# The head of a four-layer kernel: order of the last turn, the weights' squares and zero passes before the first product

## The chip, the cores and the metric

The kernel runs on one core of a Trainium2 chip. The metric is device time in microseconds (us) of one execution; of the kernel before there are three timed runs, and the median counts. Besides them one execution was profiled, and all rows shown come from it. A core has TensorE (PE, with its weight loads listed as PEld), VectorE (DVE), ScalarE (ACT), GpSimd (POOL) and SyncE (SP), which issues most DMAs. Each engine works through its own instructions in order and waits on semaphores for the others.

## The reference

Two pairs of layers act on x of 2048 tokens by 448 features: attention with 16 heads of 28, then a gated MLP of 1792 columns, and the same two again with the same weights.

```python
x = A_x
x = x + _A_ref(_layernorm(x, axis=-1), A_wqkv, A_wo)
x = x + _B_ref(_layernorm(x, axis=-1), B_w_gate, B_w_up, B_w_down)
x = x + _A_ref(_layernorm(x, axis=-1), A_wqkv, A_wo)
x = x + _B_ref(_layernorm(x, axis=-1), B_w_gate, B_w_up, B_w_down)
```

`_A_ref` multiplies by `wqkv` (448 by 1344), forms softmax(q k / sqrt(28)) v for each head and multiplies by `wo`; `_B_ref` is (sigmoid(x Wg) * (x Wu)) Wd. All inputs are float32.

## The kernel before, in words

The tokens stand as 16 tiles of 128 by 448, in four blocks (`Block`) of four tiles. Every product in the projections is made of float16 parts: an operand is scaled by a power of two, its high part is the rounding to float16 and its low part the rest. A weight matrix and a block of tokens are cut along the 448 features into four slots of 128, 128, 128 and 64 rows. The fourth slot of a block holds its high part in rows 0 to 63 and its low part in rows 64 to 127 (`tail`); the weights' fourth slot holds the same 64 rows twice.

The power of two for a weight matrix comes from its sum of squares. `measure(j)` squares the matrix `j` (0 for the queries' columns, 1 keys, 2 values) on ScalarE and adds along a row into `sums`; `size(j)` adds over the partitions with a product by a matrix of ones on TensorE (the float32 product shows as two matmuls), and `powers` makes the scale `up` from it in two small VectorE instructions (L233, L235). `high_cols` is ScalarE's scaled copy to float16 (L218), `low_cols` is VectorE's rest (L221).

The head, up to the first product, is written out in the order in which each engine gets it. SyncE issues the four tiles of block 0, the first weights in four pieces (slots 0 and 1 together, slot 2, and the 64 rows of slot 3 twice), then the second weights, block 1, the third weights and blocks 2 and 3. Meanwhile `keep_busy` makes products of a zero tile into a bank that nobody reads (L248). For each tile of block 0, `stats` (L435 to L440, VectorE and GpSimd) takes mean and spread, `scale` normalizes it (L283, VectorE) and `turn` transposes it on TensorE into four banks (L448), one for each slot. The first weights are squared in two parts of two slots each (L549), and both parts are added up by `size(0)` (L554, L556), which stands between the last tile's `scale` and its `turn`. Then come `tables()` (constants on GpSimd), the high part of the first 128 columns, `turned_high` (the block's high part out of the banks, ScalarE, L466 and L468), the high part of the other 320 columns, the low part of the first 128, `turned_low` (the block's low part, VectorE, L473 and L476) and one more zero pass.

`project` follows: seven products of 128 columns of queries and keys, each of 11 matmuls (L497) by `by_features`. The 11 terms are (high weights, high block), (high weights, low block) and (low weights, high block) for three slots, and two for the tail. Their order is a list; for the first two of the seven it is another one, since their operands become ready one after another. Behind each of the seven stands one piece of further work from `along`: behind the first `tile0` (the low part of the other 320 columns, `measure(1)`, ones for the values on GpSimd), behind the second `tile1` (`size(1)` and 64 columns of the second weights), then `tile2` (the rest of them), `measure(2)`, `size(2)` and `split_v` (the third weights). Each product is then scaled out of its bank by ScalarE (L673, L676) and VectorE (L674, L678).

## Time and profile before

| | us |
|---|---|
| median of three timed runs | 1931.62 |
| lowest and highest | 1931.43, 1933.78 |
| the profiled execution | 1932.95 |
| its span | 1930.8 |
| TensorE busy in the span | 1915.8 |
| VectorE busy | 1248.2 |
| ScalarE busy | 1314.0 |

A row of the order of time gives the start in the span and the duration in us, the engine, the line, the operation, what it writes and reads, and how many like instructions it stands for; in square brackets stands how long the engine was idle before it and what released it. Rows that group a form give its count, its busy time in us and the mean of one in ns. Rows of waits give the engine and line that waited, for whom, the total in us, the number of times and the longest.

### The profile page before, as it was taken

Reading aid. Unit: us, or ns where it says so; the run is one execution under the profiler, and the core shown is the slowest. Engines: PE = TensorE matmul, PEld = TensorE weight load, DVE = VectorE, ACT = ScalarE, POOL = GpSimd, SP = SyncE. Lnnn points to the kernel's source line nnn. Section 1 sums busy time; section 2 is a strip of 40 time slices with the busy share of each in tenths; the row PEclk is TensorE's granted clock in tenths of the full one; section 3 lists DMA queues with packets and bytes.
Section 4 is the critical chain, followed back from the end, with each engine's and each line's share of the span. In section 5 each row is a group of like instructions: output and inputs, shape, how many; then the busy total and the mean of one; then the engine's idle time right before and its main releaser. Section 6 shows DMA issues by size and latency. Waiting matters only on the chain. (4 is left out here: it accounts for less than half of the span.)

```text
span 1930.8 us, 53585 instructions
## 1 busy us (share of the span) xinstructions
PE 1915.8 (99%) x23392; PEld 1327.5 (69%) x23392; DVE 1248.2 (65%) x2348; ACT 1314.0 (68%) x1574; POOL 164.5 (9%) x308
## 2 busy tenths in 40 slices
PE   8999999999999999999999999999999999999999
PEld 4455555555566777777744568799898777777776
DVE  6638878778676555555574487787778664655543
ACT  5569999999983344444345799999999544343432
POOL 2013322221001000000000000000000000000000
PEclk9999999999999999999999999999999999999999
DMA  5566664334216313232334321122111243333310
GB/s 172 158 197 176 187 195 129 107 102 113 64 62 242 107 69 108 81 128 79 101 111 131 94 51 47 30 51 51 42 36 65 104 169 117 107 111 97 115 49 20
DMA packets 90533, 201.49 MB, mean 104 GB/s; under 512 B 10830, under 2 KB 58030, under 8 KB 90160
## 3 DMA queue, kind: packets, MB, share of 16 engines
q1 hardware_dynamic: 65680, 111.02, 19.7%
q0 software_dynamic: 17776, 83.51, 13.0%
q8 instruction: 185, 3.03, 0.7%
q10 hardware_dynamic: 6832, 3.44, 0.7%
q14 instruction: 60, 0.49, 0.1%
HBM read 142.61 MB, written 47.98 MB: 99 GB/s over the span
## 5 line engine op out<-in xcount | busy, mean ns | idle before, releaser
L1065 ACT ACTIVATE prob_s<-sc 128x1536 f32<-128x1536 f32 x658 | 890.8, 1490 | 8.6 <-PE sc L1050 6.0
L1101 PE MATMUL acc<-prob_s,val_s 128*32 128x256 f32 (+3 forms) x7732 | 591.6, 383 | 0.0
L1050 PE MATMUL sc<-qp_s 114*32 114x512 f16 x7888 | 575.8, 379 | 0.9 <-ACT prob_s L1065 0.9
L512 PEld LDWEIGHTS <-gu_s 128*128 128x128 f16 x4368 | 427.3, 98 | 60.7 <-issue 1.3
L1050 PEld LDWEIGHTS <-qp_s 114*32 114x32 f16 x8192 | 315.8, 95 | 173.0 <-issue 80.0
L1101 PEld LDWEIGHTS acc<-prob_s,val_s 128*32 128x32 f32 x7732 | 321.5, 110 | 96.2 <-issue 7.0
L1354 DVE TENSOR_TENSOR one_q<-side,one_q 128x512 f32<-128x512 f32 x112 | 71.9, 683 | 298.0 <-PE side L512 298.0
L512 PE MATMUL chain<-xwide_s,gu_s 128*128 128x256 f16 x2016 | 247.5, 273 | 0.6 <-ACT one_q L1338 0.5
L1338 ACT COPY one_q<-chain 128x256 f32<-128x256 f32 x224 | 83.0, 372 | 205.5 <-PE chain L512 201.6
L1081 DVE SCALAR_TENSOR_TENSOR power_q<-power_q,expo_q 128x512 f32<-128x512 f32 x228 | 157.8, 692 | 7.8
L1307 PE MATMUL dnp<-dn_s,hhl_q 128*128 128x448 f16 x448 | 157.9, 352 | 0.0
L1308 PE MATMUL dnp<-dn_s,hhl_q 128*128 128x448 f16 x448 | 157.9, 352 | 0.0
L1309 PE MATMUL dnp<-dn_s,hhl_q 128*128 128x448 f16 x448 | 157.9, 352 | 0.0
L512 PE MATMUL side<-xshort_s,gu_s 128*128 128x256 f16 x1120 | 140.9, 272 | 0.0
L497 PE MATMUL qkp<-xhl_s,wqk_s 128*128 128x512 f16 x616 | 139.8, 383 | 0.4 <-ACT xhl_s L466 0.3
L497 PEld LDWEIGHTS <-wqk_s 128*128 128x128 f16 x616 | 60.6, 99 | 71.5 <-issue 2.7
L1130 DVE STREAM_TRANSPOSE oturned_q<-acc 128x512 f32<-128x512 f32 x32 | 22.9, 716 | 130.9 <-PE acc L1101 130.8
L512 PE MATMUL side<-xwide_s,gu_s 128*128 128x256 f16 x672 | 91.7, 273 | 0.0
L1101 PE MATMUL acc<-power_q,val_s 128*32 128x128 f32 (+3 forms) x284 | 88.6, 394 | 0.0
L1338 ACT COPY two_q<-chain 128x256 f32<-128x256 f32 x112 | 41.7, 372 | 67.4 <-PE chain L512 67.4
L1365 ACT ACTIVATE one_q<-one_q 128x512 f32<-128x512 f32 x56 | 35.3, 630 | 59.5 <-DVE one_q L1354 59.5
L1075 DVE TENSOR_SCALAR expo_q<-aside,base 128x512 f32<-128x512 f32 x76 | 56.8, 748 | 28.7 <-PE aside L1050 28.4
(188 smaller groups left out, 2080.0 us busy)
## 6 DMA issues: line engine op xcount, KB each, us to landing
gu_s<-gu_parts POOLq DMA_DIRECT2D x56, 800.0 KB, 4.9
qp_s<-qk_scr SPq DMA_DIRECT2D x96, 224.0 KB
gu_s<-gu_parts SPq DMA_DIRECT2D x20, 800.0 KB
qk_scr<-qkhl_q SPq DMA_DIRECT2D x56, 256.0 KB
gu_parts<-pack_s POOLq DMA_DIRECT2D x14, 800.0 KB, 3.9
xraw_s<-xt_scr SPq DMA_DIRECT2D x12, 768.0 KB
xt_scr<-xs_s SPq DMA_DIRECT2D x34, 224.0 KB
qp_s<-qk_scr SPq DMA_DIRECT2D x64, 112.0 KB
```

The source lines that it names most:

```text
L497: nc.tensor.matmul(pm, w, x, start=(i == 0), stop=(i == len(terms) - 1))
L512: nc.tensor.matmul(pm, a, x, start=(first and i == 0), stop=(i == len(terms) - 1), skip_group_check=True)
L1050: nc.tensor.matmul(ps[32 * j:32 * j + 32, :], hd.k[:, keys], hd.q[:, qb * W:(qb + 1) * W], start=True, stop=True, tile_position=(0, 32 * j))
L1065: nc.scalar.activation(prob[:, 0:n, :], ps[:, 0:n, :], AF.Exp, scale=exp_scale)
L1075: nc.vector.tensor_scalar(y, ps, base2[:, 0:1], -126.0, op0=ALU.mult, op1=ALU.max)
L1081: nc.vector.scalar_tensor_tensor(p, p, c[k], y, op0=ALU.add, op1=ALU.mult)
L1101: nc.tensor.matmul(acc[qb * VC:(qb + 1) * VC, s], v[:, kc % TB, h, :], probs[c * NB + qb][:, s], start=(kc == 0 and a == 0), stop=(kc == N ...
L1307: nc.tensor.matmul(pm, hl[:, 0, s], dw[:, 0, :], start=begin, stop=False)
L1308: nc.tensor.matmul(pm, hl[:, 0, s], dw[:, 1, :], start=False, stop=False)
L1309: nc.tensor.matmul(pm, hl[:, 1, s], dw[:, 0, :], start=False, stop=end)
L1338: nc.scalar.copy(to, pm)
L1354: nc.vector.tensor_tensor(one[m], side[m], one[m], op=ALU.add)
```

## The change

The fourth turn comes ahead of the weights' sums. The first weights' squares are taken in three parts with a column of `first_sums` each: slots 0 and 1 and then slot 2 on ScalarE, slot 3 on VectorE (one instruction that multiplies and adds up, with a read of its accumulator); each part has its own product with the matrix of ones into the same bank. Zero passes stand behind every turn and around the three sums: one behind the fourth turn, three, one and three behind the sums, where one stood behind the last turn. The block's high parts come out of the banks ahead of the scaled weights: slot 0 by VectorE, slots 1 and 2 by ScalarE; the tail follows after the first 128 columns. Those columns are scaled in two steps, slot 0 alone and then the other three, and their low part stands between the block's low parts. The first product's list puts the block's low part of slots 0 and 1 ahead of the low weights, and that of slot 2 behind them. `measure` and `size` lose their special case.

```diff
-    rest = cpool.tile([P, 1], F32, name="rest")
+    first_sums = cpool.tile([P, 3], F32, name="first_sums")
...
-        def turned_high(self):
-            for kt, pt in self.pt.items():
-                if kt < 3:
-                    nc.scalar.copy(self.hi[:, kt, :], pt)
+        def turned_high(self, kts=range(4), engine=None):
+            for kt in kts:
+                if kt not in self.pt:
+                    continue
+                to, pt = ((self.hi[:, kt, :], self.pt[kt]) if kt < 3 else
+                          (self.tail[0:64], self.pt[kt][0:64]))
+                if engine is nc.vector:
+                    nc.vector.tensor_copy(to, pt)
                 else:
-                    nc.scalar.copy(self.tail[0:64], pt[0:64])
+                    nc.scalar.copy(to, pt)
...
         if first_tile == 0:
-            terms = terms[0::3] + terms[2::3] + terms[1::3] + tails
+            terms = terms[0::3] + terms[1:5:3] + terms[2::3] + terms[7:8] + tails
...
+        def measure_first(self, i):
+
+            rows = self.raw[0][:, (slice(0, 2), slice(2, 3), slice(3, 4))[i]]
+            junk = qrt.get("junk", [P, 2, D], BF16)
+            out, to = junk[:, 0:rows.shape[1]], first_sums[:, i:i + 1]
+            if i == 2:
+                nc.vector.tensor_tensor_reduce(out, rows, rows, 1.0, 0.0, op0=ALU.mult,
+                                               op1=ALU.add, accum_out=to)
+            else:
+                nc.scalar.activation(out, rows, AF.Square, accum_out=to)
+            qrt.put(junk)
+
+        def sum_first(self, i):
+            if i == 0:
+                self.first = bank(3, "sums")[:, 0:1]
+            nc.tensor.matmul(self.first, ones, first_sums[:, i:i + 1], start=(i == 0),
+                             stop=(i == 2))
+            if i == 2:
+                powers(0, 1, self.first)
...
-        def high_cols(self, j, c0, c1):
+        def high_cols(self, j, c0, c1, kts=slice(0, 4)):
             c = slice(j * D + c0, j * D + c1)
-            scaled_high(self.qk[0][:, :, c], self.raw[j][:, :, c0:c1], j)
+            scaled_high(self.qk[0][:, kts, c], self.raw[j][:, kts, c0:c1], j)
...
-    wq.measure(0)
+    wq.measure_first(0)
...
         first.scale(t)
-        if t == TB - 1:
-            wq.size(0)
         first.turn(t)
-        if t < TB - 1:
-            keep_busy()
+        keep_busy()
         if t + 2 < TB:
             first.stats(t + 2)
+    wq.sum_first(0)
+    first.turned_high([0], nc.vector)
+    keep_busy(3)
+    wq.measure_first(1)
+    wq.measure_first(2)
+    wq.sum_first(1)
+    first.turned_high([1, 2])
+    keep_busy()
+    wq.sum_first(2)
     tables()
-    wq.high_cols(0, 0, P)
+    keep_busy(3)
+    wq.high_cols(0, 0, P, slice(0, 1))
+    wq.high_cols(0, 0, P, slice(1, 4))
+    first.turned_high([3])
+    wq.high_cols(0, P, D)
+    first.turned_low([0, 1])
+    wq.low_cols(0, 0, P)
+    first.turned_low([2, 3])
     big.put(first.xn)
-    first.turned_high()
-    wq.high_cols(0, P, D)
-    wq.low_cols(0, 0, P)
-    first.turned_low()
-    keep_busy()
```

More of the change, by code (lines that the diff above doesn't have):

```diff
@@ L461, in turn_raw, with turned_low @@
             big.put(self.xn)
-        def turned_high(self):
-            for kt, pt in self.pt.items():
-                if kt < 3:
-                    nc.scalar.copy(self.hi[:, kt, :], pt)
-                else:
-                    nc.scalar.copy(self.tail[0:64], pt[0:64])
-        def turned_low(self):
-            for kt, pt in self.pt.items():
+        def turned_high(self, kts=range(4), engine=None):
[6 more added lines that the diff above has]
+                    nc.vector.tensor_copy(to, pt)
+                else:
+                    nc.scalar.copy(to, pt)
+        def turned_low(self, kts=range(4)):
+            for kt in kts:
+                if kt not in self.pt:
+                    continue
+                pt = self.pt[kt]
                 if kt < 3:
@@ L542, in read @@
             load_rows(self.raw[j], wqkv, j * D, D, parted=(j == 0))
+        def measure_first(self, i):
[15 more added lines that the diff above has]
+                powers(0, 1, self.first)
         def measure(self, j):
             junk = big.get("junk", [P, 4, D], BF16)
-            for s, to in (((slice(0, 2), sums[:, 0:1]), (slice(2, 4), rest)) if j == 0 else
-                          ((slice(0, 4), sums[:, j:j + 1]),)):
-                nc.scalar.activation(junk[:, s], self.raw[j][:, s], AF.Square, accum_out=to)
+            nc.scalar.activation(junk, self.raw[j], AF.Square, accum_out=sums[:, j:j + 1])
             big.put(junk)
         def size(self, j):
-            pb = bank(7 if j else 3, "sums")
-            nc.tensor.matmul(pb[:, 0:1], ones, sums[:, j:j + 1], start=True, stop=(j > 0))
-            if j == 0:
-                nc.tensor.matmul(pb[:, 0:1], ones, rest, start=False, stop=True)
+            pb = bank(7, "sums")
+            nc.tensor.matmul(pb[:, 0:1], ones, sums[:, j:j + 1], start=True, stop=True)
             powers(j, 1, pb[:, 0:1])
-        def high_cols(self, j, c0, c1):
+        def high_cols(self, j, c0, c1, kts=slice(0, 4)):
             c = slice(j * D + c0, j * D + c1)
-            scaled_high(self.qk[0][:, :, c], self.raw[j][:, :, c0:c1], j)
+            scaled_high(self.qk[0][:, kts, c], self.raw[j][:, kts, c0:c1], j)
         def low_cols(self, j, c0, c1):
```

## The prediction

> **What bounds the kernel now.** I read the page's first, second and fourth parts, then the order of time over the first 36 us, then stretches of it with the granted clock.

> ```profile
> span 1930.8 us, 53585 instructions
> PE 1915.8 (99%) x23392; PEld 1327.5 (69%) x23392; DVE 1248.2 (65%) x2348; ACT 1314.0 (68%) x1574; POOL 164.5 (9%) x308
> PE 44%; DVE 0%; ACT 0%; issue 0%; DVEq 0%; ACTq 0%
> ```

> TensorE is busy for 99% of the span and is nearly alone on the chain that ended last. So what reaches the first product earlier, or makes the first products faster, shortens the run by as much, provided no later wait is tied to a fixed time. The execution took 1932.95 us, of which the span is 1930.8; it lies 1.33 above the median of the timed runs, 1931.62.

> The order of time (start, duration, engine, line, operation) shows the front as a relay across four engines:

> ```profile
> 9.61 0.51 DVE L283 TENSOR_SCALAR xn_s<-x,mv,rs 128x448 f32<-128x448 f32 x1 [0.72 <-POOL rs L440]
> 10.52 0.19 ACT L549 ACTIVATION_READ_ACCUMULATOR junk_s<-wraw_s 128x1 f32 x1
> 10.85 0.35 PE L554 MATMUL sums<-sums,ones 128*128 128x1 f32 x2 [1.03 <-POOL ind_f_q L181]
> ...
> 11.40 0.95 ACT L549 ACTIVATE junk_s<-wraw_s 128x896 bf16<-128x896 f32 x1 [0.69 <-DMA wraw_s<-in_A_wqkv_dram]
> 12.49 0.58 PE L556 MATMUL sums<-rest,ones 128*128 128x1 f32 x2 [1.29 <-ACT junk_s L549]
> 12.94 1.09 PE L448 MATMUL turn<-ident,xn_s 128*128 128x128 f32 x4
> 13.11 0.16 DVE L233 TENSOR_SCALAR pw<-sums 128x1 int32<-128x1 int32 x1 [3.00 <-PE sums L556]
> 13.49 0.72 ACT L218 ACTIVATE wqk_s<-wraw_s,up 128x512 f16<-128x512 f32 x1 [1.05 <-DVE up L235]
> 14.12 1.54 ACT L466 CAST xhl_s<-turn 128x512 f16<-128x512 f32 x3
> 14.25 0.75 DVE L221 SCALAR_TENSOR_TENSOR wqk_s<-wraw_s,up,wqk_s 128x512 f16<-128x512 f32 x1 [0.79 <-ACT wqk_s L218]
> 14.74 7.10 PE L497 MATMUL qkp<-xhl_s,wqk_s 128*128 128x512 f16 x22 [0.28 <-ACT xhl_s L466]
> 14.92 1.88 DVE L473 TENSOR_TENSOR xhl_s<-turn,xhl_s 128x512 f16<-128x512 f32 x3
> ...
> 21.68 0.28 PE L554 MATMUL sums<-sums,ones 128*128 128x1 f32 x2
> 21.82 4.91 PE L497 MATMUL qkp<-xhl_s,wqk_s 128*128 128x512 f16 x22
> 22.00 0.16 DVE L233 TENSOR_SCALAR pw<-sums 128x1 int32<-128x1 int32 x1 [0.91 <-PE sums L554]
> ```

> The last piece of the first weights lands at 11.40 (ScalarE waits for it). Square, sum on TensorE, scale on VectorE and ScalarE's scaled copy follow one another; the fourth turn stands behind the sums, at 12.94, though its input was ready at 10.12. The first product starts at 14.74. The first 22 products take 7.10, the next 22 take 4.91. The sums of the second weights at 21.68 stand behind those 22, and all scaling of the second weights hangs on them, so 21.68 is the mark that I move.

> Why 7.10 is seen in stretches (busy us of PE, PEld, DVE, ACT, POOL with instruction counts, granted clock, DMA share, GB/s):

> ```profile
> 5.44:8.85 3.41, 1.74 (x10) 0.97 (x10) 2.69 (x7) 0.00 (x0) 1.82 (x5) 1.00 1.05 311
> 8.85:12.26 3.41, 1.22 (x7) 0.78 (x7) 0.55 (x2) 1.91 (x4) 3.11 (x10) 1.00 1.11 258
> 12.26:15.67 3.41, 2.90 (x9) 1.55 (x10) 1.73 (x5) 2.36 (x7) 2.93 (x8) 0.50 0.99 306
> 15.67:19.08 3.41, 3.41 (x9) 1.13 (x8) 3.35 (x4) 3.40 (x4) 0.60 (x3) 0.50 1.13 324
> 19.08:22.50 3.42, 3.42 (x19) 1.74 (x18) 1.28 (x5) 1.35 (x3) 0.00 (x0) 1.00 1.00 374
> ```

> From 12.26 to 19.08 the clock is half, after a stretch in which TensorE was busy 1.22 of 3.41. The first 4.3 us of products run in it.

> **The change part by part.** Loads are issued in the same order on SyncE and no DMA is added or moved; GpSimd's order is unchanged, since nothing that moved waits for it. The rest is 7 zero passes, one more sum, a smaller split of squares and another order.

> *Squares.* SyncE issues a later load when the third slot's semaphore comes free; the last tail's landing is ScalarE's wait to 11.40.

> ```profile
> 10.40 0.47 SPq L200 DMA_DIRECT2D wraw_s<-in_A_wqkv_dram  x1
> L953 DVE CUSTOM_DVE_ANT_0 junk_s<-raw_s,sums x19: 1144/1284/2085, 146.9 to 223.4; 128x1024 bf16<-128x1024 f32 x14, 128x1792 bf16<-128x1792 f32 x4, 128x896 bf16<-128x896 f32 x1
> L953 DVE DVE_READ_ACCUMULATOR2_ANT part<- 128x1 f32 x19 | 1.6, 82 | 0.0
> ```

> So slot three is there by 10.40, and ScalarE, free at 10.71, squares it then: 896 columns cost 0.95 (at 11.40) and 1792 cost 1.69 (at 17.29, below), so 448 cost 0.58, and with the read it is done at 11.40. The tails go to VectorE from 11.40. Its multiply-and-sum is L953's operation: 1.14 for 896 (the shortest of 19) and 2.08 for 1792, so 0.68 for 448, plus 0.08: ready at 12.16. Before, TensorE had the squares at 12.49. Bounds for the 0.68: 0.5 (the pass over 448 columns at 9.61) to 1.14 (the row of twice the columns).

> *Turn and zero passes.* The turn starts at 10.15 instead of 12.94.

> ```profile
> 1.25 3.60 PE L248 MATMUL still<-still_q 128*128 128x512 f16 x8 [1.25 <-DVE warm L166]
> 8.95 0.65 PE L448 MATMUL turn<-ident,xn_s 128*128 128x128 f32 x4 [0.51 <-DVE xn_s L283]
> 9.44 0.38 PE L248 MATMUL still<-still_q 128*128 128x512 f16 x1
> ```

> At full clock it takes 0.65, with the zero pass from 0.49 on. TensorE keeps order, so everything behind it counts: turn 10.15, pass, first sum (0.35, as at 10.85) to 11.2, three passes at 4.91/22 = 0.22 to 11.87, second sum 12.2, one pass 12.45, third sum. Its data are there at 12.16, so by data VectorE reads it at 12.5 (0.32 from 21.68 to 22.00), by queue at 12.85. I take 12.7. The passes behind it (0.67) end at 13.4, before anything needs TensorE. In the stretch to 12.26 TensorE is now busy for 0.87 + 0.87 + 0.35 + 0.67 + 0.3 = 3.1 of 3.41. The stretch to 8.85 kept the clock with 1.74 of 3.41 us, the next one lost it with 1.22. So I take the full clock as held up to the first product and behind it.

> [...]

> *First product.* Scales and handover: 13.11 to 13.49, 0.38, so ScalarE starts at 13.08. It now scales only the first slot, 128 columns.

> ```profile
> 16.02 1.37 ACT L218 ACTIVATE wqk_s<-wraw_s,up 128x1280 f16<-128x1280 f32 x1
> 16.83 0.68 DVE L476 TENSOR_TENSOR xhl_s<-turn,xhl_s 64x512 f16<-64x512 f32 x1
> 17.29 1.69 ACT L549 ACTIVATE junk_s<-wraw_s 128x1792 bf16<-128x1792 f32 x1
> 17.55 1.55 DVE L221 SCALAR_TENSOR_TENSOR wqk_s<-wraw_s,up,wqk_s 128x1280 f16<-128x1280 f32 x1
> 22.38 0.51 ACT L218 ACTIVATE wqk_s<-wraw_s,up 128x256 f16<-128x256 f32 x1 [1.61 <-DVE up L235]
> ```

> 0.51 for 256 and 1.37 for 1280 give 0.40 for 128: done 13.48. The copy of the turned slots no longer stands between, as VectorE (slot 0, at 10.45, at most the 0.63 of a low part, before the tails land) and ScalarE (slots 1, 2, from 11.4 to 12.4 at 0.51 each) did them while the sums were under way. First product at 13.55, 1.2 earlier. Bounds, with those above: 13.3 to 14.0.

> *The 22 products.* At 0.22 they would take 4.9, but now VectorE sets the pace: from 13.05 two low parts at 0.63, low columns 0.75 (14.25), a third low part 0.63, the tail 0.70: 16.4. ScalarE's part (three slots 0.61, the tail's copy 0.51, then 1.37) ends at 15.7 and does not hold it. The two tail products end at 16.9; seven of the second tile take 1.56, to 18.45, when the low columns (16.4 + 1.55 = 17.95) are there; four more, 19.35. So the second weights' sums come at 19.35 instead of 21.68: **2.3 us**, 1.2 from the earlier start and 1.1 from the products. The full clock alone is worth 2.2 there (half of 14.74 to 19.08); the waits for VectorE take 1.1 of it back.

> *Cover.* The squares of the second weights now start on ScalarE at 15.6 instead of 17.29 and must end by 19.35; they take 1.9, so 1.8 are spare. If their weights landed only at 17.29, the copy of the first tile would be late by 0.4 and nothing else. Everything from 21.68 on hangs on that sum and shifts as a whole. One wait in this stretch is 1.1 long, on VectorE's split of the third weights:

> ```profile
> PE vp L523 <- DVE wv_s L221: 1.1, 1, 1.1
> 26.55 1.68 ACT L549 ACTIVATE junk_s<-wraw_s 128x1792 bf16<-128x1792 f32 x1
> ```

> It follows the products too, so it moves along; it does not shrink.

> *Sum.* 1932.95 - 2.3 = 1930.65 against the profiled execution. How much of its excess over the median is profiling and how much its own half-clock stretch can't be read: if it is all profiling, the median becomes 1929.3; if the timed runs have less half clock, they gain less. I take the middle: **1929.9**.

> **The rivals.**

> *The clock wanders* (part of the forecast's own range). The timed runs differ by 2.35 us among themselves (1931.43 to 1933.78), about the 2.2 that the half clock costs here. In a timed run with the flips up to 2 us later or earlier, the half clock costs the first products 1 us less or more than the 2.2 here (half of 4.3), so the gain is 1.3 to 3.3: 1928.3 to 1930.3 from the median. [...]

> *All waits of the front fall away*: data set the third sum (12.5), the low parts overlap, 22 products take 4.9 from 13.3, and the sums come at 18.2, 3.5 earlier; with half of the 1.1 wait gone too, 4.0: 1927.6. For it: VectorE was idle for 3.0 us ahead of 13.11. Against it: its five pieces add up to 3.3.

> *Slower: the zero passes at half clock.* If the clock is half from 10 us on (it was half at 1.25 to 4.85, 0.43 a pass), the same queue takes: turn 1.09, pass 0.43, sum 0.58, three passes 1.28, sum 0.58, pass 0.43, sum 0.58: third sum read at 15.0, three passes more to 16.3, first product 1.6 later than before. If the clock comes back at 19.08 as before, 6.5 products run at 0.43 and 15.5 at 0.22: 22.5 against 21.68, 1932.4 from the median; it is slower from a return at about 17.3 on. If it never comes back within the 22, 16.3 + 9.4 = 25.7: 4.0 later, 1935.6. Against it: the rows at 8.95 and 9.44 are at full speed, and what falls between them and 10.15 is unchanged.

> *It moves the front and gives it back*: a load at a fixed time. The third weights are squared at 26.55, 24.2 then. The hardware queue's packets and MB, over the first 9 and the first 18 us:

> ```profile
> q1 hardware_dynamic: 1211, 1.96, 77.4%
> q1 hardware_dynamic: 2359, 4.61, 92.1%
> ```

> 1.96 MB had moved by 9 us, and the first 1.835 MB (four tiles of x, 0.917, and the first weights, as much) had landed by 11.40. 4.61 MB by 18 us are the 4.59 up to the third weights, so by the same lag they land at about 21, 3 us early. Should they land at 26.5, up to 2.3 are lost again: 1931.6.

> **How the numbers follow.** Forecast, with the wandering clock: 0.62. All waits gone: 0.12. Slower by the passes: 0.11. Given back: 0.15. A measurement of this kernel tells about 0.2%, 3.9 us, from no change. Beyond it on the fast side is the second case alone, with a little of the first: 0.13; on the slow side half of the third: 0.06; within: 0.81. The forecast's own range is 1928.3 to 1930.7; with the given-back case and the nearer half of the slower one, and cutting the far ends, 1927.9 to 1932.3 leaves out about 2 in 10.

> **What would show it.** The fourth turn at 10.1 to 10.3; a third sum between 12.2 and 12.6; the first product at 13.3 to 13.8; full clock in the stretches to 12.26, 15.67 and 19.08; VectorE without idle time from 13.05 to 18; the sums of the second weights at 19.2 to 19.5; from there every row earlier by the same amount. A half clock in any of these stretches, a multiply-and-sum above 1.2 us, a DMA as the releaser of ScalarE at 15.6, or a longer wait on the third weights' split would make it wrong.

## The result, and the profile after

| | before | after |
|---|---|---|
| median, us | 1932.62 (22 runs, 1931.43 to 1934.1) | 1929.72 (22 runs, 1929.09 to 1932.98) |
| the profiled execution | 1932.95 | 1929.57 |
| its span | 1930.8 | 1927.9 |

The ratio of the times is 0.9986, with a 95% interval of 0.998 to 0.9993: 2.9 us between the medians, about 0.15%, with an interval that leaves out 1. The kernel before was timed again beside the new one, which moved its median from 1931.62 to 1932.62.

The order of time of the changed kernel, the rows that answer to those shown of before (start, duration, engine, line, operation, idle time ahead in brackets):

```profile
8.01 0.95 ACT L560 ACTIVATE junk_q<-wraw_s 128x896 bf16<-128x896 f32 x1 [5.71 <-DMA wraw_s<-in_A_wqkv_dram]
9.74 0.66 PE L448 MATMUL turn<-ident,xn_s 128*128 128x128 f32 x4 [0.35 <-DVE xn_s L283]
10.11 0.69 DVE L470 CAST xhl_s<-turn 128x512 f16<-128x512 f32 x1 [0.42 <-PE turn L448]
10.67 0.81 PE L248 MATMUL still<-still_q 128*128 128x512 f16 x3
10.71 0.61 DVE L557 CUSTOM_DVE_ANT_0 junk_q<-wraw_s 128x448 bf16<-128x448 f32 x1
11.25 0.08 DVE L557 DVE_READ_ACCUMULATOR2_ANT first_sums<- 128x1 f32 x1
11.31 0.28 PE L566 MATMUL sums<-first_sums,ones 128*128 128x1 f32 x2
11.53 0.38 PE L248 MATMUL still<-still_q 128*128 128x512 f16 x1
11.74 0.28 PE L566 MATMUL sums<-first_sums,ones 128*128 128x1 f32 x2
12.06 0.16 DVE L233 TENSOR_SCALAR pw<-sums 128x1 int32<-128x1 int32 x1 [0.72 <-PE sums L566]
12.44 0.91 ACT L218 ACTIVATE wqk_s<-wraw_s,up 128x128 f16<-128x128 f32 x2 [1.15 <-DVE up L235]
12.89 2.46 PE L504 MATMUL qkp<-xhl_s,wqk_s 128*128 128x512 f16 x9
...
15.63 2.97 PE L504 MATMUL qkp<-xhl_s,wqk_s 128*128 128x512 f16 x13 [0.28 <-DVE xhl_s L483]
...
18.43 0.28 PE L578 MATMUL sums<-sums,ones 128*128 128x1 f32 x2
...
32.86 0.35 PE L530 MATMUL vp<-wv_s,xhl_s 128*128 128x448 f16 x1 [1.07 <-DVE wv_s L221]
```

The row of the kernel before that answers to the last one:

```profile
36.11 0.35 PE L523 MATMUL vp<-wv_s,xhl_s 128*128 128x448 f16 x1 [1.08 <-DVE wv_s L221]
```

The fourth turn has moved from 12.94 to 9.74, the first product from 14.74 to 12.89, and the sums of the second weights from 21.68 to 18.43, 3.25 earlier. The span is 2.9 shorter. The wait on the third weights' split is as long as before (1.07 against 1.08) and 3.25 earlier: nothing between was given back. (The span less the start of those sums is 1909.12 before, 1909.47 after, and between 1908.1 and 1909.5 in the other profiles, so the 0.35 is scatter.) Three things in these rows are not the change's doing or not as planned. The first weights' slots were there at 8.01 instead of 9.66, in the same order of loads. The square of the last piece, at 10.71, names no DMA and starts as VectorE ends its copy of slot 0 (10.11): here the weights were no longer what the head waited for (the trace records the last of their transfers as landed at 9.95). And TensorE's queue shows: the last square is read out at 11.33, but the third sum runs at 11.74, behind the second sum and its pass.

Stretches of the changed kernel (busy us of PE, PEld, DVE, ACT, POOL, then the granted clock, DMA share and GB/s):

```profile
8.85:12.26 3.41, 3.06 (x21) 2.19 (x20) 1.91 (x6) 1.83 (x6) 3.20 (x9) 1.00 1.09 309
12.26:15.67 3.41, 2.89 (x13) 0.86 (x12) 3.35 (x7) 3.23 (x5) 2.93 (x8) 1.00 1.01 371
15.67:19.08 3.41, 3.41 (x18) 1.72 (x18) 2.74 (x5) 2.20 (x4) 0.60 (x3) 1.00 1.11 350
```

TensorE is busy for 3.06 of the stretch in which it had 1.22, and the clock stays full, where it was half for 6.82 us.

### The profile page after: what moved, and what is told of

Its sections match the earlier page's. It is cut to its first block, busy times and chain, and to the rows that moved or that the text cites. A ratio compares the mean times of both kernels' runs of the same rounds, so it can differ in the third digit from the quotient of the medians.

```text
span 1927.9 us, 53606 instructions
## 1 busy us (share of the span) xinstructions
PE 1915.1 (99%) x23401; PEld 1297.4 (67%) x23401; DVE 1249.7 (65%) x2351; ACT 1313.1 (68%) x1574; POOL 164.9 (9%) x308
## 5 line engine op out<-in xcount | busy, mean ns | idle before, releaser
L1123 PE MATMUL acc<-prob_s,val_s 128*32 128x256 f32 (+3 forms) x7732 | 582.8, 383 | 0.0
L1072 PE MATMUL sc<-qp_s 114*32 114x512 f16 x7888 | 567.1, 379 | 0.9 <-ACT prob_s L1087 0.9
L1072 PEld LDWEIGHTS <-qp_s 114*32 114x32 f16 x8192 | 295.7, 96 | 188.7 <-issue 91.7
L1123 PEld LDWEIGHTS acc<-prob_s,val_s 128*32 128x32 f32 x7732 | 304.6, 110 | 108.8 <-issue 7.9
```

Of the source, the lines that this page charges most:

```text
L1072: nc.tensor.matmul(ps[32 * j:32 * j + 32, :], hd.k[:, keys], hd.q[:, qb * W:(qb + 1) * W], start=True, stop=True, tile_position=(0, 32 * j))
L1123: nc.tensor.matmul(acc[qb * VC:(qb + 1) * VC, s], v[:, kc % TB, h, :], probs[c * NB + qb][:, s], start=(kc == 0 and a == 0), stop=(kc == N ...
```

## The experiments

Two questions: does the gain come from the held clock, from the order, or from both; and what in the order carries it. Times are medians of 11 runs, each beside runs of the kernel before on the same chip (1932.41 for the first four, 1932.43 for the next four, 1931.94 for the last three). Since loads land at another time in each execution (the last piece of the first weights at 11.40 and 10.32 in two profiles of the kernel before), the profiles are compared by the **lag**: the start of the second weights' sums, less the start of the square that takes the last piece of the first weights. It is 21.68 - 11.40 = 10.28 before and 18.43 - 10.71 = 7.72 after. Where the row of that square names a DMA, the lag starts as the piece lands; where it doesn't (10.71 above, and three more profiles below), VectorE was still at its copy of slot 0, and the piece had landed earlier.

### Without the added passes

```diff
     wq.sum_first(0)
     first.turned_high([0], nc.vector)
-    keep_busy(3)
...
-    keep_busy()
     wq.sum_first(2)
     tables()
-    keep_busy(3)
```

> The changed kernel without its seven added zero passes; the pass behind the fourth turn stays. Theory (earlier start and held clock each carry part of the 2.9 us): the fourth turn still comes ahead of the sums, but the clock falls to half between 11 and 13 us, the sums take 0.58 instead of 0.28, the first product starts 0.3 to 0.6 later than with the passes and some ten products run at 0.43, so 1.5 to 2.5 us are lost: 1931.2 to 1932.2. Rival A (the clock carries everything): 1932.6, as before. Rival B (order alone carries it, the passes are idle): within 0.3 of 1929.7, with full clock up to the first product.

Measured: 1930.57 (1929.55 to 1932.21), ratio 0.9988 [0.9979, 0.9997]. Its order of time and its stretches:

```profile
11.45 0.63 DVE L557 CUSTOM_DVE_ANT_0 junk_q<-wraw_s 128x448 bf16<-128x448 f32 x1 [1.00 <-DMA wraw_s<-in_A_wqkv_dram]
13.40 7.91 PE L504 MATMUL qkp<-xhl_s,wqk_s 128*128 128x512 f16 x22 [0.88 <-ACT wqk_s L218]
21.14 0.28 PE L578 MATMUL sums<-sums,ones 128*128 128x1 f32 x2
```

```profile
9.15:12.56 3.41, 2.23 (x14) 1.42 (x12) 1.52 (x4) 2.56 (x6) 3.15 (x7) 1.00 1.09 285
12.56:15.97 3.41, 2.57 (x6) 0.83 (x7) 3.34 (x7) 3.02 (x5) 2.57 (x9) 0.50 1.01 352
15.97:19.39 3.42, 3.42 (x9) 1.18 (x8) 2.03 (x3) 2.26 (x4) 0.00 (x0) 0.50 1.10 314
```

The first product comes 1.95 after the square, no later than with the passes (12.89 - 10.71 = 2.18), where it was 14.74 - 11.40 = 3.34 before: the order alone gives the earlier start. The clock then falls for two stretches, 22 products take 7.91, and the lag is 9.69. In the timed runs the granted clock over the whole run was below 1.000 in 10 of 11, against 4 of 22 with the passes. The loss, 0.85 against 1929.72, is smaller than expected: the profiled execution, 1931.97, is one of the two longest, and I had charged a late start that does not occur. Five of the 11 runs lie below 1930, though four of these had lost the clock, so a lost clock doesn't cost the same in every run. Neither rival holds.

### The passes alone

```diff
         if t == TB - 1:
+            keep_busy(4)
             wq.size(0)
...
             if j == 0:
+                keep_busy(4)
                 nc.tensor.matmul(pb[:, 0:1], ones, rest, start=False, stop=True)
...
     first.turned_low()
-    keep_busy()
+    keep_busy(3)
```

> The kernel before with zero passes alone: four ahead of the first sum, four between the two sums, three behind the last turn instead of one; order, squares and scaling as before. Theory: full clock to the first product and behind it, the sums 0.3 and the turn 0.4 faster, first product at about 14.3 instead of 14.7, and 22 products paced by VectorE, so 1.3 to 1.9 us gained: 1930.7 to 1931.3. Rival A (the clock carries everything): 1929.7. Rival B (order alone): 1932.6.

Measured: 1930.64 (1930.02 to 1931.0), ratio 0.9989 [0.998, 0.9998]. Its order of time:

```profile
11.12 0.95 ACT L549 ACTIVATE junk_s<-wraw_s 128x896 bf16<-128x896 f32 x1 [0.57 <-DMA wraw_s<-in_A_wqkv_dram]
14.26 2.64 PE L497 MATMUL qkp<-xhl_s,wqk_s 128*128 128x512 f16 x9 [0.52 <-ACT xhl_s L466]
17.09 2.96 PE L497 MATMUL qkp<-xhl_s,wqk_s 128*128 128x512 f16 x13 [0.18 <-DVE xhl_s L476]
19.89 0.28 PE L554 MATMUL sums<-sums,ones 128*128 128x1 f32 x2
```

The granted clock was 1.000 in 10 of 11 runs, where the kernel before beside it had it in none of 33. The lag is 8.77, and the time lies just under the expected span. The first product still comes 3.14 after the square (3.34 in the first profile of the kernel before, 3.14 in the second, shown below), but 22 products are through in 5.6. So the passes alone are worth 1.8 us (1932.41 - 1930.64). The order alone, in the experiment above, is worth as much (1932.41 - 1930.57). Together they give 2.9, less than the sum of both, so they overlap: to a kernel with the passes the order adds 0.92, to a kernel with the order the passes add 0.85 (from these medians to 1929.72). Of the 22 runs of the changed kernel 18 lie at or below 1930.1; here 10 of 11 lie above.

### The turn alone

```diff
         first.scale(t)
-        if t == TB - 1:
-            wq.size(0)
         first.turn(t)
...
             first.stats(t + 2)
+    wq.size(0)
```

> The kernel before with the fourth turn moved ahead of the weights' sums and nothing else. Theory: the turn is not what the first product waits for, so the start moves by at most 0.2, and TensorE is busy for about 1.9 of the 3.4 us in which the clock was lost, instead of 1.2. If transposes count as activity the clock may hold for another stretch and up to 2 us are gained (1930.6); if they don't, the clock falls as before and the time is within 0.4 of 1932.6. I expect the second. The rival that order carries the gain expects 1931.5 or less with the clock still falling.

Measured: 1931.48 (1930.9 to 1934.01), ratio 0.9995 [0.9986, 1.0004], so not told from no change, though the median lies 0.9 below, more than I expected, and by 0.02 inside what the rival had named. Its order of time and its stretches:

```profile
10.65 0.95 ACT L549 ACTIVATE junk_s<-wraw_s 128x896 bf16<-128x896 f32 x1 [0.77 <-DMA wraw_s<-in_A_wqkv_dram]
13.79 6.58 PE L497 MATMUL qkp<-xhl_s,wqk_s 128*128 128x512 f16 x22 [1.42 <-ACT xhl_s L466]
20.21 0.28 PE L554 MATMUL sums<-sums,ones 128*128 128x1 f32 x2
```

```profile
10.27:13.68 3.41, 1.14 (x9) 0.85 (x8) 0.69 (x3) 2.17 (x5) 3.09 (x5) 1.00 1.04 314
13.68:17.10 3.42, 3.31 (x8) 1.05 (x8) 3.36 (x6) 3.42 (x6) 1.84 (x9) 0.50 1.10 347
```

The first product comes 3.14 after the square, as in the second profile of the kernel before: the turn was not what it waited for, and the rival's reason, an order that starts the products earlier, isn't there. The clock falls all the same (below 1.000 in all 11 runs), here for one stretch instead of two. Whether the earlier turn shortens the half clock or this execution only met the stretches otherwise is left open, as the next run shows that they move by themselves; so is what a turn counts for the clock.

### The kernel before once more

> The kernel before once more, for a second profile. [...] The last piece of the first weights lands within 0.8 us of 11.4.

One run, 1932.21. Its order of time and its stretches:

```profile
10.32 0.95 ACT L549 ACTIVATE junk_s<-wraw_s 128x896 bf16<-128x896 f32 x1 [0.56 <-DMA wraw_s<-in_A_wqkv_dram]
13.46 6.88 PE L497 MATMUL qkp<-xhl_s,wqk_s 128*128 128x512 f16 x22 [0.95 <-ACT xhl_s L466]
20.18 0.28 PE L554 MATMUL sums<-sums,ones 128*128 128x1 f32 x2
```

```profile
10.57:13.98 3.41, 1.50 (x9) 0.93 (x10) 1.32 (x4) 2.56 (x6) 3.10 (x5) 1.00 1.01 334
13.98:17.39 3.41, 3.41 (x9) 1.07 (x9) 3.35 (x5) 3.41 (x4) 1.50 (x8) 0.50 1.13 347
```

The same kernel: the last piece lands at 10.32 instead of 11.40, further off than I expected, and the clock is half from 13.98 to 17.39, one stretch of 3.41, instead of 12.26 to 19.08, two of them. The stretches are not tied to the kernel's start. The lag is 9.86, so two profiles of one kernel differ by 0.42 in it.

The span here is 1929.6, 1.2 below the first profile's, while the time is only 0.74 below: 2.61 of the time lies outside the span, against 2.15 there. In 11 of the 33 runs of the kernel before beside the first four experiments this part is over 1.9, in none of the 33 runs of the changed kernel. What it is, the record doesn't say; the medians of the spans differ by about as much as those of the times (2.65 and 2.69 against those 33).

### Two squares instead of three

```diff
-            rows = self.raw[0][:, (slice(0, 2), slice(2, 3), slice(3, 4))[i]]
+            rows = self.raw[0][:, (slice(0, 2), slice(2, 4))[i]]
...
     wq.measure_first(1)
-    wq.measure_first(2)
...
     keep_busy()
-    wq.sum_first(2)
     tables()
```

> The changed kernel with the first weights squared in two parts of two slots on ScalarE, as before; the third sum and VectorE's square are gone, the passes stay. Theory: the squares are done 0.3 later (0.95 and its read instead of 0.68 and its read), ScalarE copies slots 1 and 2 after them and so starts the scaled copy late by up to 1.0: 0.3 to 1.0 lost, 1930.0 to 1930.7. Rival (the split is hidden by the passes' queue on TensorE): no loss, 1929.7.

Measured: 1929.55 (1928.07 to 1931.11), ratio 0.9984 [0.9975, 0.9993]. Its order of time:

```profile
11.21 0.95 ACT L560 ACTIVATE junk_q<-wraw_s 128x896 bf16<-128x896 f32 x1 [0.65 <-DMA wraw_s<-in_A_wqkv_dram]
12.72 0.16 DVE L233 TENSOR_SCALAR pw<-sums 128x1 int32<-128x1 int32 x1 [1.40 <-PE sums L566]
19.10 0.28 PE L578 MATMUL sums<-sums,ones 128*128 128x1 f32 x2
```

No loss in the time, as the rival said. The rows say less for its reason. From the square's start to the scale's first step it is 1.51, against 1.35 in the profile after, where the queue of passes held the third sum, but against 1.11 in the second profile of the changed kernel (10.88 to 11.99, below), where it didn't. So by the rows the third part is worth 0.2 to 0.4 there; the medians don't show it.

### Twice the passes, and fewer

```diff
-    keep_busy(3)
+    keep_busy(6)
...
-    keep_busy()
+    keep_busy(2)
     wq.sum_first(2)
     tables()
-    keep_busy(3)
+    keep_busy(6)
```

> The changed kernel with twice the passes around the sums: six, two and six instead of three, one and three. Theory (the passes hold the clock already, and TensorE's order makes more of them delay the third sum): four passes more ahead of the third sum cost 0.4 to 0.9, the three more behind it 0 to 0.4: 1930.1 to 1931.0. Rival (the clock is held only in part of the executions, and more passes hold it in all): the slowest runs near 1932 to 1933 vanish and the median falls to 1929.5 or less.

> The changed kernel with two, none and two passes around the sums instead of three, one and three. Theory: the third sum no longer stands behind a pass and a late second sum, 0.2 to 0.5 gained where the clock holds (1929.2 to 1929.5), but more executions lose the clock and lie 2 to 3 us higher. Rival (three, one and three are needed): the median rises to 1931 or more.

The second kernel has `keep_busy(2)` in both outer places and none in the middle. Measured: 1929.98 (1929.11 to 1931.52) and 1929.39 (1928.62 to 1933.29). The scale's first step and the first product with six, two and six passes, and the scale's first step with two, none and two:

```profile
13.08 0.16 DVE L233 TENSOR_SCALAR pw<-sums 128x1 int32<-128x1 int32 x1 [1.23 <-PE sums L566]
14.28 2.11 PE L504 MATMUL qkp<-xhl_s,wqk_s 128*128 128x512 f16 x9
```

```profile
12.40 0.16 DVE L233 TENSOR_SCALAR pw<-sums 128x1 int32<-128x1 int32 x1 [0.47 <-PE sums L566]
```

VectorE's idle time ahead of the scale is 1.23 with twice the passes, so their queue is seen. It is 0.72 after (12.06) and 0.47 with fewer, but the step between these two isn't shown to be the queue's: the second profile of the changed kernel has 0.47 as well (11.99, below). With twice as many the clock was 1.000 in all 11 runs, against 18 of 22, a difference that 11 runs can't tell from chance, and no run lies above 1931.52; the median is 0.26 higher, less than the 0.4 that I expected, and not the gain that the rival named. With fewer, 10 of 11 kept the clock, so that more executions would lose it is not shown.

### The order of the low parts

```diff
-    first.turned_low([0, 1])
     wq.low_cols(0, 0, P)
-    first.turned_low([2, 3])
+    first.turned_low()
...
-            terms = terms[0::3] + terms[1:5:3] + terms[2::3] + terms[7:8] + tails
+            terms = terms[0::3] + terms[2::3] + terms[1::3] + tails
```

> The changed kernel with the low columns ahead of all the block's low parts again, and the first product's terms in the order of before. Theory: VectorE's five pieces take 3.3 us in any order and the tail comes last in both, so the end of the second tile moves by less than 0.3: 1929.5 to 1930.0. Rival (the order of the low parts carries part of the gain): 0.5 or more lost, 1930.2 or above.

Measured: 1930.55 (1929.91 to 1932.25), ratio 0.999 [0.9981, 0.9999]. Its order of time:

```profile
10.57 0.61 DVE L557 CUSTOM_DVE_ANT_0 junk_q<-wraw_s 128x448 bf16<-128x448 f32 x1
13.23 0.75 DVE L221 SCALAR_TENSOR_TENSOR wqk_s<-wraw_s,up,wqk_s 128x512 f16<-128x512 f32 x1 [0.97 <-ACT wqk_s L218]
19.36 0.28 PE L578 MATMUL sums<-sums,ones 128*128 128x1 f32 x2
```

The lag is 8.79, 1.07 more than after, and the median 0.83 more; 10 of 11 runs lie above 1930.1, where 4 of 22 did. The rival is right. From the scale's first step (11.92 here, 12.06 after) the low part of the tail, VectorE's last before the second product's, starts 3.89 later here (15.81) and 2.83 after (14.89): VectorE's order carries 1.06 of the 1.07, and next to nothing is left for the list of terms. My expectation counted VectorE's pieces and forgot its idle time: the low columns must wait for ScalarE's scaled copy, 0.97 here, and in the changed kernel the first two low parts fill that hole.

### The changed kernel and two others side by side

The second kernel is the one with fewer passes. The third has, besides, the first three terms of the second product ahead of the first one's tail terms:

```diff
...
+                        product(pm, 0, range(9), 0)
+                        product(second, 1, range(3), 1)
+                        product(pm, 0, range(9, 11), 0)
...
```

> The changed kernel once more, beside the next two on one chip. Theory: the last piece of the weights lands between 10.3 and 11.5, the sums of the second weights come 7.5 to 7.8 after it (7.7 before), and the median is 1929.3 to 1930.2, with a few runs 2 to 3 us above that lost the clock.

> The kernel with two, none and two passes once more. Theory (a pass and the second sum delay the third sum by 0.3, and nothing else changes while the clock holds): 0.2 to 0.4 below the changed kernel on the same chip. Rival (the queue of passes costs nothing, as the weights' landing sets the third sum): within 0.1 of it.

> The kernel with two, none and two passes, and the first three terms of the second product of 128 columns put ahead of the first one's two tail terms. Theory (VectorE's low part of the tail holds TensorE there for 0.28): that wait goes and 0.2 to 0.3 more are gained. Rival (VectorE's low columns, not the tail, set the end of the second product): the wait moves to the low weights' terms and nothing is gained.

Measured: 1929.23, 1929.54 and 1929.30, ratios 0.9987 [0.9977, 0.9996], 0.9989 [0.998, 0.9998] and 0.9988 [0.9979, 0.9998]. The rows of the three, in this order:

```profile
7.17 1.06 PE L448 MATMUL turn<-ident,xn_s 128*128 128x128 f32 x4
10.88 0.62 DVE L557 CUSTOM_DVE_ANT_0 junk_q<-wraw_s 128x448 bf16<-128x448 f32 x1 [0.24 <-DMA wraw_s<-in_A_wqkv_dram]
11.99 0.16 DVE L233 TENSOR_SCALAR pw<-sums 128x1 int32<-128x1 int32 x1 [0.47 <-PE sums L566]
12.83 2.46 PE L504 MATMUL qkp<-xhl_s,wqk_s 128*128 128x512 f16 x9 [0.20 <-ACT wqk_s L218]
18.36 0.28 PE L578 MATMUL sums<-sums,ones 128*128 128x1 f32 x2
```

```profile
11.03 0.72 DVE L557 CUSTOM_DVE_ANT_0 junk_q<-wraw_s 128x448 bf16<-128x448 f32 x1
18.61 0.28 PE L578 MATMUL sums<-sums,ones 128*128 128x1 f32 x2
```

```profile
10.81 0.61 DVE L558 CUSTOM_DVE_ANT_0 junk_q<-wraw_s 128x448 bf16<-128x448 f32 x1
12.74 5.36 PE L505 MATMUL qkp<-xhl_s,wqk_s 128*128 128x512 f16 x22 [0.42 <-ACT wqk_s L218]
17.93 0.28 PE L579 MATMUL sums<-sums,ones 128*128 128x1 f32 x2
```

Lags 7.48, 7.58 and 7.12. The changed kernel's lag and median lie just under the expected spans. One run of 11 (1931.45) lies 2 us above the rest, but its clock is given as 1.000, while the one run that lost it by this figure took 1929.67: so my theory that the long runs are those that lost the clock is not borne out here. Fewer passes gain nothing measurable on the same chip (0.31 more, where 0.2 to 0.4 less was expected), so the 0.33 between 1929.39 and 1929.72 isn't shown to be an effect of them. The last kernel no longer has the wait of 0.28 ahead of the tail terms and its lag is the shortest of all, but its time can't be told from that of the other two.

The first row shows what the clock's figure leaves out. The turn at 7.17 takes 1.06, where it takes 0.66 in the profile after and 1.09 at half clock, yet the clock of that stretch is given as 1.00. In this profile TensorE ran at half speed up to about 9.5 us (a turn of 1.06 at 8.45, one of 0.60 at 9.64), and came to full speed in time for the sums (0.28 at 10.29). The second profile of the kernel before shows the half speed as well (a turn of 1.09 at 7.12). So a run's 1.000 says that no fall was recorded; it doesn't say that the head ran at full speed from the start. Three of the 26 runs of the kernel before beside these three have 1.000 as well and took 1931.35 to 1932.76.

## Why the prediction came out

**The time** lies 0.2 from the forecast and inside the range, but by luck, a balance of two errors. The gain was worked out as 2.3 and was 2.9 between the medians (2.7 in the last comparison). And the 1.33 by which the profiled execution lay above the median shown was mostly the luck of three runs: over 22 it is 0.33. Taking half of it off (the middle between 1929.3 and 1930.65 is 1930.0, not 1929.9) happened to make up for the gain that was too small. From the last piece's square to the mark the gain was sized well: the lag fell from 10.28 and 9.86 to 7.72 and 7.48 in two profiles each, by 2.1 to 2.8. What the medians gained beyond that isn't accounted for by itself; it lies within the scatter of the loads and of the rest of the kernel.

**The start.** The fourth turn, the third sum, the first product and the second weights' sums all came earlier than the times that were to show the forecast: 9.74, 11.74, 12.89 and 18.43, against 10.1, 12.2, 13.3 and 19.2 at the earliest. Measured from the start of the last piece's square, the front ran where the working put it: 2.15 to the first product were predicted (13.55 - 11.40), 2.18 and 1.95 measured (after, and again), against 3.34 before. Of the 1.16 between 3.34 and 2.18 the shorter scaled copy and the copies moved out of its way are worth 0.80 (from ScalarE's first scaled copy to the first product 1.25 before, 0.45 after), the way from the square to that copy 0.36. Neither the early copies nor the scaling in two steps was run alone. What failed is the landing itself, taken as fixed at 11.40. It was 11.40 and 10.32 in two profiles of the kernel before, and 10.88 in the second of the kernel after, with the same loads in the same order; in the profile after it was earlier still, and the fourth turn and VectorE's copy set the square's start.

VectorE's square took 0.61 for the predicted 0.68. The bound of 1.14 was not needed.

**The queue of passes** was sized at 0 to 0.35 for the third sum, and I took half. After, it was 0.41 by start (11.33 to 11.74). In the second profile, with a later landing, VectorE's wait was as short as with fewer passes, 0.47, and as without the added ones (0.47 there too). So three and one passes were seen to cost something only where the weights came early.

**The clock.** No fall is recorded in 18 of 22 runs, and the profile has full clock up to the first product and behind it; the four other runs took 1930.44 to 1932.98. The passes, not the order, do that: with the passes alone no fall is recorded in 10 of 11, with the order alone in 1 of 11. But the rule that I read from the stretches, 1.74 of 3.41 keeps the clock and 1.22 loses it, is too simple: without the passes it was lost after a stretch with 2.23. What decides isn't shown by busy time, nor by the longest gap: of the 1.29 that end at 12.49 only 1.06 lie ahead of the fall at 12.26, without the passes the longest in the stretch to 12.56 was 0.60 and the clock fell, and in the kernel before the stretch to 8.85 has one of 0.88 and kept it.

**VectorE as the pace of the first two products** is right, and a little over-sized: 12.89 to 18.43 is 5.54, where 5.8 was predicted and 4.9 would be without waits. The wait of 0.28 ahead of the tails is in the rows, and the experiment with VectorE's other order, which makes the same products take 6.61 (12.75 to 19.36), shows that VectorE sets the pace.

**The rivals.** The wandering clock is real: one kernel, two profiles, half clock for 6.82 and for 3.41 us. It was put into the forecast's own range, which is where it belongs. The 2 us by which it let the flips move was an estimate with no run behind it; in the second profile the fall came 1.72 later and the end 1.69 earlier. Passes at half clock around the sums are in no profile, so what they would cost is open; of the four runs with a recorded fall three lie below the median of before and one 0.4 above. All waits gone did not come, though the mark at 18.43 looks like it: that rival put it at 18.2, the forecast at 19.35. From the square's start it is 7.72 and 7.48, against 6.8 for the rival and 7.95 for the forecast, so the early mark comes of the earlier start of that square. Nor was anything given back, as the third weights' wait moved along unchanged.

## What to carry to other kernels

Here the relay across engines at the head was worth its reordering (2.9 us between the medians) although TensorE is busy for 99% of the span, but what is won is found by lags from the event that sets it (here mostly the landing of the weights), not by times from the start; look in each profile whether that event still sets it. Filler work on TensorE held the clock through the waits here (no fall recorded in 18 of 22 runs, against 1 of 11 without the added passes) and can cost its place in the queue (VectorE's wait ahead of the scale was 1.23 with twice the passes, 0.72 and 0.47 in the two profiles of the changed kernel): put it where data are late, and look at what stands behind it. Before calling an order of equal work neutral, look for the hole that one of its pieces must wait in (0.97 ahead of the low columns in the other order here).

## What the runs showed of the hardware

The half speed at the start lasts differently long as well: in the first profiles of both kernels eight passes from 1.25 us on take 3.60 and 3.59, or 0.45 each, where the three at 10.67 in the profile after take 0.27 each, and turns take 0.66 from 5.8 us on, in the kernel before up to the fall; in the second profiles turns take 1.06 and more up to 9.3 at least.

Loads of the same sizes in the same order from the start of the kernel landed up to 1.1 us apart (11.40 and 10.32 for the last piece of the first weights). It is as large as what a single step of this change is worth. The rest of the kernel, from the second weights' sums to the end, scatters as much (1908.1 to 1909.5), and both limit how much of a change in the head 11 runs can tell.
